# Four buffers for values, seven for gated halves, whole rows of weights, and a new order of the work, in an attention and gating kernel on one core

## The chip, the core and the metric

The kernel runs on one core of a Trainium2 chip. A core has five engines, each with its own stream of instructions: TensorE (PE in the views, its weight loads PEld), VectorE (DVE), ScalarE (ACT), GpSimd (POOL) and SyncE (SP), which here issues the DMAs. They wait for each other by semaphores alone. The metric is the device time of one execution in microseconds (us).

## The reference

Attention over B=4 batches, H=8 heads, S=768 positions and 64 elements a head, in which a query sees the first `n_global` = 8 keys and the last `n_local` = 96, with a bias that grows with distance; then a convolution of 5 taps, a sigmoid gate and two products with 512x512 weights:

```python
scores = q @ k.T / 8 - slope[h] * dist          # only kept keys
a = softmax(scores);  x = a @ v                 # heads side by side: x is [4, 768, 512]
gate = sigmoid(sum_k conv_w[k] * x[t - 4 + k])
out = (gate * (x @ w_val)) @ w_out
```

Inputs `w_val`, `w_out` and `conv_w` come as 64-bit floats, the rest and the output as 32-bit.

## The kernel before

Work is cut into 32 groups g of (batch, half of the sequence, pair of heads); a group has 3 blocks of 128 queries, in all 96 steps s. Four groups make a phase ph, a half sequence of a batch over all 512 features. For a group: `L` loads keys and queries (tile kq), `LV` loads values (va); `S` (L631) multiplies them on PE into sb; `AM` (L639) adds the bias and takes the minimum on DVE; `EX` (L650) is the exponential on ACT; `RG`, `RC` and `NM` (L657, L661, L669 or L667) divide by the sum; `PT` (L682) transposes p on PE into a PSUM bank pt or x; `EV` copies that to ab; `PV` (L709, L716) multiplies by the values, two groups at a time, into x. Then `XS` copies x to xs, `XH` and `XL` split it into a rounded and a rest part (xh, xl), `CV` (L807, L811, L809) makes the gate in five taps and `SG` (L842) its tanh. For a phase, `VM` (L849) makes val from xh, xl and the weights, three matmuls for each pair of column blocks; `GM` (L856) multiplies val by the gate; `GH` and `GL` (L863) split that into gh and gl; `OM` (L872) multiplies them with the second weights into o; `OE` (L884, L886) scales o into ob, and `ST` stores it.

The weights are taken apart from 64 to two 32-bit parts first: `WL` loads one of eight tiles of 128 rows (L534), `WA`, `WZ`, `W2` to `W4`, `WH`, `WS`, `WD` and `WP` do the arithmetic. At the end `FA`, `FB` and `FC` (L943, L947, L953 to L959) reduce the row minima to one flag: should the inputs not fit the window of this fast path, a general path runs after it. It does not run here.

Nothing is scheduled on the chip or by the framework: `SLOTS` gives each operation a number, `ENGINES` the engine for those that can run on several, and `Plan.order` writes the instructions out by that number. On an engine they run strictly in that order, SP's loads too. `plan.ring(tag, n, ...)` makes an operation that needs one of n buffers depend on the one that frees it; so `LV` of group g waits for the `PV` that used its buffer last, and `WL` of tile i for `W4` of tile i-2.

Of the kernel before, what the change touches and what calls it, by code (L numbers as in the profile page):

```python
# [17 lines left out]
RAW_B, XH_B, GATE_B, P_B, T_B, A_B, V_B, W_B, WT_B = 4, 7, 2, 7, 8, 5, 6, 2, 2  # L18
X_B, S_B, XS_B = 2, 2, 8
# [31 lines left out]
    "CWL": (14,),  # L51
    "CWA": (113,),
    "CW": (136,),
    "S0": (8,),
# [1131 lines left out]
```

## Time and profile before

| | before |
|---|---|
| median of 3 runs | 256.35 us (255.11 to 257.29) |
| profiled execution | 255.96 us, of which the span from first to last instruction is 254.2 us |
| TensorE matmuls | busy 244.3 us, 96% of the span, x3381 |
| TensorE weight loads | busy 206.1 us, x3381 |
| VectorE, ScalarE, GpSimd | busy 218.3, 197.3 and 136.2 us |
| DMA | 36.35 MB, 143 GB/s over the span |
| granted TensorE clock | 0.998 of full speed |

A busy share says how much of the time an engine had an instruction under way; matmuls overlap, so a busy PE need not be at its peak. An idle stretch of an engine is put down to what ended it ("releaser"); "issue" means that nothing the profile knows of ended it. Queue q8 in the DMA table is PE's stream of instructions, fetched from memory in packets.

### The profile page before, as it was taken

The numbers are of one execution on the slowest core, as the hardware profiler recorded it, in microseconds if no ns is written. First come the engines' busy times: TensorE is split into PE (matmuls) and PEld (weight loads), VectorE is DVE, ScalarE is ACT, GpSimd is POOL, SyncE is SP. The second block draws the span as 40 slices with busy tenths as digits, with TensorE's granted clock in tenths as the row PEclk, the third lists the DMA queues.
The fourth block names the chain that finished last, engine by engine and source line by source line (L and its number), as shares of the span: only waits on it lengthen the run. The fifth ranks groups of instructions, "written<-read, shape, count | busy, mean of one in ns | idle before, by whom it ended". The sixth has DMA issues, their size and how long they took to land.

```text
span 254.2 us, 8955 instructions
## 1 busy us (share of the span) xinstructions
PE 244.3 (96%) x3381; PEld 206.1 (81%) x3381; DVE 218.3 (86%) x768; ACT 197.3 (78%) x670; POOL 136.2 (54%) x228
## 2 busy tenths in 40 slices
PE   8898989999999999999999999999999999999992
PEld 3457757887789988899889988999899879878982
DVE  4998989999999999999999999988889777766820
ACT  4999979999998999899697989496769759333321
POOL 5797979997869554186604483055253703402110
PEclk9999999999999999999999999999999999999999
DMA  5977997736615762370826371173320003020103
GB/s 158 370 206 235 315 401 241 251 108 195 204 61 163 259 186 65 109 240 12 279 78 205 122 233 59 41 221 118 99 96 3 4 0 126 1 85 0 41 3 129
DMA packets 16302, 36.35 MB, mean 143 GB/s; under 512 B 1920, under 2 KB 4480, under 8 KB 16256
## 3 DMA queue, kind: packets, MB, share of 16 engines
q1 hardware_dynamic: 16112, 35.75, 42.3%
q8 instruction: 27, 0.44, 0.7%
q14 instruction: 19, 0.16, 0.2%
q10 hardware_dynamic: 144, 0.00, 0.0%
HBM read 29.46 MB, written 6.29 MB: 141 GB/s over the span
## 4 chain that ended last, share of the span: by engine, by line
PE 85%; ACT 5%; DVE 3%; POOL 2%; issue 1%; DMA 1%; ACTq 0%; POOLq 0%; DVEq 0%
PE val L849 27%; PE o L872 26%; PE sb L631 10%; PE x L716 9%; PE x L709 5%; PE pt L682 4%; ACT p L650 3%; PE x L682 3%; POOL p L669 1%; DMA counts_i<-in_counts 1%; ACT ab L298 1%; PE pt L544 1%; DVE t L639 1%; POOL sm L657 1%; DVE ob L886 1%
## 5 line engine op out<-in xcount | busy, mean ns | idle before, releaser
L650 ACT ACTIVATE p<-t,mins 128x168 f32<-128x168 f32 (+1 forms) x192 | 80.9, 425 | 6.3 <-PE pt L682 2.6
L807 DVE SCALAR_TENSOR_TENSOR gate<-xs,cwt,gate 128x384 f32<-128x384 f32 x128 | 82.8, 662 | 1.6 <-POOL gate L811 1.0
L639 DVE CUSTOM_DVE_ANT_0 t<-sb,bias 128x168 f32<-128x168 f32 (+1 forms) x192 | 54.5, 315 | 5.0 <-PE sb L631 4.9
L669 POOL TENSOR_SCALAR p<-p,rs 128x168 f32<-128x168 f32 (+1 forms) x86 | 49.7, 589 | 14.9 <-ACT p L650 5.7
L849 PE MATMUL val<-xh,wvh 128*128 128x384 f32 x128 | 45.2, 353 | 0.0
L849 PE MATMUL val<-xh,wvl 128*128 128x384 f32 x128 | 43.2, 337 | 0.0
L849 PE MATMUL val<-xl,wvh 128*128 128x384 f32 x128 | 43.2, 337 | 0.0
L872 PE MATMUL o<-woh,gh 128*128 128x512 f32 (+1 forms) x100 | 40.1, 401 | 0.0
L631 PEld LDWEIGHTS sb<-kq 64*64 64x64 f32 x1088 | 30.9, 134 | 10.5 <-issue 7.1
L872 PE MATMUL o<-wol,gh 128*128 128x512 f32 (+1 forms) x100 | 38.7, 387 | 0.0
L872 PE MATMUL o<-woh,gl 128*128 128x512 f32 (+1 forms) x100 | 38.5, 385 | 0.0
L631 PE MATMUL sb<-kq 64*64 64x104 f32 (+3 forms) x1088 | 36.1, 265 | 1.2 <-DMA kq<-in_kq 1.1
L650 ACT ACTIVATION_READ_ACCUMULATOR p<-t,mins 128x1 f32 x192 | 36.9, 192 | 0.0
L667 ACT ACTIVATE p<-p,rs 128x168 f32<-128x168 f32 (+1 forms) x72 | 28.8, 428 | 3.8 <-DVE rs L661 3.7
L657 POOL TENSOR_SCALAR sm<-sm 128x4 f32<-128x4 f32 (+2 forms) x30 | 9.8, 326 | 39.3 <-ACT p L650 37.0
L863 POOL TENSOR_TENSOR gl<-g,gh 128x384 fp32r<-128x384 f32 x17 | 18.5, 1091 | 16.1 <-ACT gh L298 15.7
L849 PEld LDWEIGHTS val<-xh,wvh 128*128 128x128 f32 x128 | 24.1, 188 | 2.6 <-issue 0.5
L799 POOL TENSOR_TENSOR xl<-xs,xh 128x384 fp32r<-128x384 f32 x18 | 20.2, 1120 | 9.3 <-ACT xh L298 7.8
L716 PE MATMUL x<-ab,va 104*64 104x128 f32 (+1 forms) x384 | 24.7, 277 | 0.0
L849 PEld LDWEIGHTS val<-xl,wvh 128*128 128x128 f32 x128 | 24.1, 188 | 0.4
L298 ACT COPY ab<-pt 128x384 f32<-128x384 f32 (+3 forms) x41 | 19.4, 481 | 6.1 <-PE pt L682 6.1
L849 PEld LDWEIGHTS val<-xh,wvl 128*128 128x128 f32 x128 | 24.1, 188 | 0.0
(162 smaller groups left out, 424.1 us busy)
## 6 DMA issues: line engine op xcount, KB each, us to landing
...
```

The source lines that it names most:

```text
L298: nc.scalar.copy(dst, src)
L631: nc.tensor.matmul(s[rows, u : u + w], T["rq", g][r, k * P + half * QH : k * P + (half + 1) * QH], T["rk", g][r, c : c + w], start=True, s ...
L639: nc.vector.tensor_tensor_reduce(out=t[:, :n], in0=T["s", s // HB, s % HB, j][:, :n], in1=bias[:, h, :P] if n == P else bias[:, h, P:], op ...
L650: nc.scalar.activation(T["p", s][:, j, :n], T["t", s, j][:, :n], AF.Exp, bias=mins[:, s, j : j + 1], scale=-1.0, accum_out=T["sm", batch_o ...
L667: nc.scalar.mul(pr, pr, rs)
L669: engine(e).tensor_scalar(out=pr, in0=pr, scalar1=rs, scalar2=1.0, op0=ALU.mult, op1=ALU.mult)
L716: nc.tensor.matmul(T["x", g][rows(i), c0 : c0 + P], T["near", g][:n, k, j], T["a", HB * g + k][:n, j * P : (j + 1) * P], start=False, stop ...
L799: engine(e).tensor_sub(tile_of(("xl", g), [P, HT], F32R, "xl", XH_B), xs[g % XS_B][:, HIST:], T["xh", g])
L807: nc.vector.scalar_tensor_tensor(out=gt, in0=src, scalar=w, in1=gt, op0=ALU.mult, op1=ALU.add)
L849: nc.tensor.matmul(T["val", ph, m], (wvh, wvh, wvl)[r][:, m, c * P : (c + 1) * P], (T["xh", g], T["xl", g], T["xh", g])[r], start=(c == 0 ...
L863: engine(e).tensor_sub(tile_of(("gl", ph, m), [P, HT], F32R, "gl", 5), T["g", ph, m], T["gh", ph, m])
L872: nc.tensor.matmul(T[key][:, cols], (T["gh", ph, c], T["gl", ph, c], T["gh", ph, c])[r][:, rows], (woh, woh, wol)[r][:, c, cols], start=(c ...
```

## The change

It has five parts. (1) The order `SLOTS` and the engines `ENGINES` are new numbers throughout. (2) `V_B`, the buffers for values, goes from 6 to 4, and the buffers for gh and gl from 5 to 7 (`GH_B`). (3) The first weight matrix is laid out by the host so that a tile is one whole row of 4 KB in each partition, loaded by one DMA; before, two DMAs brought four pieces of 1 KB for each partition. (4) The third instruction of `distances_all` gets a second operation (times 1.0), and the function may run on POOL as well; the table keeps it on DVE. (5) 37 of the 42 `RG`, instead of 30, run on POOL, and so on: `CV` moves 7 first taps from POOL to DVE, `EV` 11 copies, `XS` 8 and `GH` 3 from ACT to DVE, `GL` 3 from DVE to POOL, `OE` 6 from DVE to ACT, `WA` 3 from POOL to ACT; `NM` is 85 on POOL, 66 on ACT, 41 on DVE (86, 72, 34 before); `XL` is 16 on DVE (14 before).

```diff
-RAW_B, XH_B, GATE_B, P_B, T_B, A_B, V_B, W_B, WT_B = 4, 7, 2, 7, 8, 5, 6, 2, 2
-X_B, S_B, XS_B = 2, 2, 8
+RAW_B, XH_B, GATE_B, P_B, T_B, A_B, V_B, W_B, WT_B = 4, 7, 2, 7, 8, 5, 4, 2, 2
+X_B, S_B, XS_B, GH_B = 2, 2, 8, 7
...
-    "WL": (5, 9, 91, 128, 174, 255, 292, 386),
+    "WL": (5, 11, 79, 127, 167, 220, 342, 369),
...
     def distances_all(e):
-        ve = nc.vector
+        ve = engine(e)
...
-        ve.tensor_scalar(out=d1[:, G], in0=m0[:, :NG], scalar1=nlf, scalar2=None, op0=ALU.add)
+        ve.tensor_scalar(out=d1[:, G], in0=m0[:, :NG], scalar1=nlf, scalar2=1.0, op0=ALU.add, op1=ALU.mult)
...
         if i < NC:
-            t = w.rearrange("p (c n) two -> p c (n two)", c=NC)
-            src = wv.bitcast(I32).rearrange("(c p) n -> p c n", p=P)[:, :, 2 * i * P : 2 * (i + 1) * P]
-            parts = [(t[:, c], src[:, c]) for c in (slice(0, NC // 2), slice(NC // 2, NC))]
+            parts = [(w, wv[:, i].bitcast(I32).rearrange("p (n two) -> p n two", two=2))]
...
-        copy(e, tile_of(("gh", ph, m), [P, HT], F32R, "gh", 5), T["g", ph, m])
+        copy(e, tile_of(("gh", ph, m), [P, HT], F32R, "gh", GH_B), T["g", ph, m])
...
-        "wv": bits(inputs["moe_w_val"]),
+        "wv": bits(np.asarray(inputs["moe_w_val"]).reshape(NC, P, NC, P).transpose(1, 2, 0, 3)).reshape(P, NC, -1),
```

What the new numbers do at two places follows. First SP's loads near the start, from just behind the fourth weight tile on (w is a tile of weights, kq and va those of a group; the names in brackets are semaphores waited for: DMAHW of an earlier transfer, the others of an engine). Before:

```order
L393 DMA va_457<-in_va 128x640 [waits DMAHW3_49]
L379 DMA kq_481<-in_kq 128x888 [waits DMAHW4_49,PE_49]
L534 DMA w_573<-in_wo 128x512 [waits DMAHW5_49,DMAHW6_49,DVE_49,Pool_49]
L534 DMA w_573<-in_wo 128x512
L393 DMA va_607<-in_va 128x640 [waits DMAHW7_49]
L379 DMA kq_628<-in_kq 128x888 [waits DMAHW0_49,PE_49]
L379 DMA kq_635<-in_kq 128x784 [waits DMAHW1_49,PE_49]
L393 DMA va_644<-in_va 128x768 [waits DMAHW2_49]
L379 DMA kq_651<-in_kq 128x784 [waits DMAHW3_49,PE_49]
L393 DMA va_661<-in_va 128x768 [waits DMAHW4_49]
L393 DMA va_671<-in_va 128x768 [waits DMAHW5_49]
```

Of the change:

```order
L394 DMA va_440<-in_va 128x640
L380 DMA kq_474<-in_kq 128x888 [waits DMAHW0_49,PE_49]
L380 DMA kq_478<-in_kq 128x888 [waits DMAHW1_49,PE_49]
L394 DMA va_485<-in_va 128x640 [waits DMAHW2_49]
L533 DMA w_561<-in_wo 128x512 [waits DMAHW3_49,DVE_49,Pool_49]
L533 DMA w_561<-in_wo 128x512 [waits DMAHW4_49]
L380 DMA kq_576<-in_kq 128x784 [waits DMAHW5_49,PE_49]
L533 DMA w_702<-in_wo 128x1024 [waits DMAHW6_49,DVE_49,Activation_49]
L380 DMA kq_755<-in_kq 128x784 [waits DMAHW7_49,PE_49]
L380 DMA kq_762<-in_kq 128x784 [waits DMAHW0_49,PE_49]
L394 DMA va_771<-in_va 128x768 [waits DMAHW1_49]
```

Behind the fifth weight tile (the first from in_wo, in two DMAs) there are now one kq and then the sixth weight tile, w_702, which waits for DVE (`W4` of the fourth tile) and holds up what stands behind it; before, three kq and four va followed, with two more va behind the last row shown. Ahead of the fifth tile the change has one kq and one va more.

Then DVE at the end, from `GM` of the last column block (g_3) on: before, these eight are the last rows of the program there, and gl_3 is made on POOL.

```order
L856 SCALAR_TENSOR_TENSOR g_3_4567<-gate_4269,val_3_4539 128x384 [waits DVE_49,PE_49,Activation_49]
L953 TENSOR_REDUCE far<-pt_89 1x1 [waits PE_49]
L954 TENSOR_SCALAR slow<-counts 1x1
L955 SCALAR_TENSOR_TENSOR slow<-counts,slow 1x1 [waits DVE_49]
L956 SCALAR_TENSOR_TENSOR slow<-counts,slow 1x1 [waits DVE_49]
L957 SCALAR_TENSOR_TENSOR slow<-far,slow 1x1 [waits DVE_49]
L958 TENSOR_SCALAR slow<-slow 1x1 [waits DVE_49]
L959 CAST flag<-slow 1x1 [waits DVE_49]
```

Of the change, from the gl before the flag:

```order
L862 TENSOR_TENSOR gl_2_4563<-g_2_4540,gh_2_4555 128x384 [waits DVE_49,Activation_49]
L952 TENSOR_REDUCE far<-pt_89 1x1 [waits PE_49]
L953 TENSOR_SCALAR slow<-counts 1x1
L954 SCALAR_TENSOR_TENSOR slow<-counts,slow 1x1 [waits DVE_49]
L955 SCALAR_TENSOR_TENSOR slow<-counts,slow 1x1 [waits DVE_49]
L956 SCALAR_TENSOR_TENSOR slow<-far,slow 1x1 [waits DVE_49]
L957 TENSOR_SCALAR slow<-slow 1x1 [waits DVE_49]
L958 CAST flag<-slow 1x1 [waits DVE_49]
L862 TENSOR_TENSOR gl_3_4580<-g_3_4561,gh_3_4569 128x384 [waits Activation_49]
```

The seven instructions of the flag now stand ahead of the last gl on the same engine. And PE of the change at the same place, from the transposition of the minima (the matmul into pt) to the matmul that takes that gl:

```order
L946 MATMUL pt_89<-ident,row_max 1x128
L871 MATMUL o_0_4557<-woh,gh_2_4555 128x512 [waits Activation_49]
L871 MATMUL o_0_4557<-woh,gl_2_4563 128x512 [waits DVE_49]
L871 MATMUL o_0_4557<-wol,gh_2_4555 128x512
L871 MATMUL o_1_4585<-woh,gh_0_4511 128x512
L871 MATMUL o_1_4585<-woh,gl_0_4518 128x512
L871 MATMUL o_1_4585<-wol,gh_0_4511 128x512
L871 MATMUL o_0_4557<-woh,gh_3_4569 128x512 [waits Activation_49]
L871 MATMUL o_0_4557<-woh,gl_3_4580 128x512 [waits DVE_49]
```

Before, the rows are the same in kind, but the matmul that takes gl_3 comes three rows later, behind the o_1 matmuls with gh_1 and gl_1, and waits for POOL.

## Rows read from the trace of the kernel before

**Rows 1.** The page's first part: busy us (share of the span) xinstructions.

```profile
PE 244.3 (96%) x3381; PEld 206.1 (81%) x3381; DVE 218.3 (86%) x768; ACT 197.3 (78%) x670; POOL 136.2 (54%) x228
```

**Rows 2.** Stretches in us: busy time (instructions) of each engine, granted clock, DMA share, GB/s.

```profile
46.00:66.60 20.60, 20.60 (x364) 16.80 (x361) 20.60 (x82) 20.32 (x72) 18.93 (x27) 1.00 0.54 172
...
75.80:127.00 51.20, 51.17 (x820) 45.25 (x820) 50.17 (x185) 45.85 (x161) 31.13 (x49) 1.00 0.51 162
127.00:240.00 113.00, 113.00 (x1365) 99.75 (x1362) 96.25 (x292) 78.85 (x253) 40.13 (x63) 1.00 0.26 86
```

**Rows 3.** Waits of PE: line, releaser, us in total, times, longest.

```profile
PE x L709 <- ACT ab L298: 1.3, 2, 0.8
PE pt L682 <- issue: 1.3, 1, 1.3
PE x L682 <- issue: 0.3, 1, 0.3
PE x L709 <- ACT p L650: 0.2, 1, 0.2
```

**Rows 4.** PE in order of time, 33 to 36 and 42 us: start, us, operation [idle before <-releaser].

```profile
32.93 0.66 PE L682 MATMUL pt<-ident,p 64*104 64x64 f32 x11
34.85 0.21 PE L682 MATMUL pt<-ident,p 64*128 64x64 f32 x1 [1.26 <-issue]
34.99 1.22 PE L631 MATMUL sb<-kq 64*64 64x168 f32 x36
...
42.41 0.33 PE L709 MATMUL x<-ab,va 64*64 64x64 f32 x4
```

**Rows 5.** Waits of DVE, then of ACT, between 30 and 37 us.

```profile
DVE t L639 <- PE sb L631: 0.9, 1, 0.9
ACT ab L298 <- PE pt L682: 1.2, 1, 1.2
```

**Rows 6.** DMA queue q8 to 32.34 us, at 32.3 to 33.4, and to 200.68: packets, MB, share.

```profile
q8 instruction: 2, 0.03, 0.4%
...
q8 instruction: 1, 0.02, 5.4%
...
q8 instruction: 23, 0.38, 0.7%
```

**Rows 7.** Stretches from 0, columns as in rows 2.

```profile
0.00:28.50 28.50, 25.04 (x362) 15.92 (x362) 23.45 (x115) 24.22 (x94) 22.16 (x56) 1.00 0.78 244
0.00:32.35 32.35, 28.89 (x452) 19.35 (x454) 27.21 (x128) 28.07 (x107) 25.78 (x61) 1.00 0.80 260
...
0.00:200.69 200.69, 195.29 (x2988) 163.40 (x2989) 185.79 (x699) 174.49 (x613) 125.11 (x215) 1.00 0.51 169
```

**Rows 8.** DMA queue of the loads, 25.7 to 32.34 us: packets, MB, share of 16 engines.

```profile
q1 hardware_dynamic: 882, 2.20, 97.4%
```

**Rows 9.** SP in order of time, 24 to 34 us.

```profile
24.32 0.80 SPq L534 DMA_DIRECT2D w<-in_wo  x2
25.17 0.43 SPq L393 DMA_DIRECT2D va<-in_va  x1
...
27.77 5.38 SPq L393 DMA_DIRECT2D va<-in_va  x4
```

**Rows 10.** DVE's groups by form: busy us, mean ns | idle us before, releasers.

```profile
L863 DVE TENSOR_TENSOR gl<-g,gh 128x384 fp32r<-128x384 f32 x15 | 8.5, 577 | 0.0
L300 DVE COPY xs<-x 128x384 f32<-128x384 f32 x5 | 2.7, 546 | 0.0
```

**Rows 11.** PE and DVE in order of time, 242 to 245 us.

```profile
242.37 0.27 PE L947 MATMUL pt<-ident,row_max 128*1 128x128 f32 x1
...
244.12 0.39 PE L872 MATMUL o<-woh,gl 128*128 128x512 f32 x1
242.68 0.28 DVE L953 TENSOR_REDUCE far<-pt 1x1 f32<-1x128 f32 x1 [0.90 <-PE pt L947]
...
244.06 0.14 DVE L959 CAST flag<-slow 1x1 int32<-1x1 f32 x1
```

More of the change, by code (lines that the diff above doesn't have):

```diff
@@ L39 @@
-    "DIST": (10, 12),
-    "BIAS": (15, 22, 18, 25, 16, 23, 13, 36),
[10 rows of a table removed]
[L51 to L54, printed above, removed]
+    "CNT": (8,),
+    "DIST": (10, 13),
+    "BIAS": (18, 22, 15, 23, 14, 36, 16, 37),
[10 rows of a table added]
+    "CWL": (7,),
+    "CWA": (109,),
+    "CW": (135,),
+    "S0": (9,),
     "S": (
-        17, 41, 72, 107, 139, 175, 217, 259, 302, 347, 402, 439, 476, 511, 570, 630, 678, 706, 763, 810, 863, 903,
-        961, 997, 1035, 1087, 1131, 1222, 1281, 1300, 1389, 1448,
+        17, 39, 68, 98, 133, 178, 209, 245, 286, 325, 398, 438, 469, 506, 571, 595, 673, 701, 760, 806, 854, 901,
+        955, 1007, 1043, 1086, 1153, 1215, 1265, 1284, 1365, 1458,
@@ L189 @@
 ENGINES = {
-    "BIAS": "SSSVGGGG",
+    "DIST": "VV",
+    "BIAS": "SSSGGVGG",
     "BI2": "GV",
-    "WA": "GGGGGGGG",
-    "WZ": "VVGGGGGG",
-    "WH": "GSSVSSSS",
-    "WD": "VVGV",
-    "WP": "VVGVSSSS",
-    "RG": "GVGGGGGGGGGGGGVGVGVGVGGGVGGGVGGGVGGVVGVGVG",
+    "WA": "SGGSGGSG",
+    "WZ": "GGGVGGGG",
+    "WH": "GSSGSSSS",
+    "WD": "GGGV",
+    "WP": "VVVVVSSS",
+    "RG": "GGGGGGGGGGGGGGGGGVGGGGGGVGGVGGGGGGGVGGGGGV",
     "NM": (
-        "SGGVGGGGGVGSSGGGGGSGGGVGGSGSGGGSGGVGGSGVGSSGGGSSGGSGSGVGSGSGSGGSSGVGGVGVGSGGVGSGSSGGSGGVSSSGVSVS"
-        "GSSVSVSGGVVSGGSGSSSGGGGGGSSSVSSVSVSVSSVVGGSVGSSGSVGSGSSSGVSSSVSGGGVSGGGGSVVVGGGGSSGVSSGSSVVSSSSS"
-    ),
-    "EV": "SSSSSSSSSVVSSSVSSSSSVSSSSSSSSSVSSSSSSSSSSVSSSSVSSSSSSSSSVSSVSSSVVSVSVSVSSSSSVSVVSSSS",
-    "XS": "SSSSSSSSSSVSSSSVSSSVSVSSSSSSSSSV",
-    "XH": "VSSGGSGSGSSVSSGGSVGVSSVSSSVSGSGG",
-    "XL": "GVVGGGVGGGGGGGVVGGGVGVVGVVGVVGVV",
+        "VGSGGVGSSGGGGGSGGSSGVVGGGVGGVGGSGGGGGSGGSSGGGGGGGSSGGSSSVSSGGGGSSSGSGVVGVVSVSVSGSGGSGGSGVGSSVGGS"
+        "VSGSVSSSSVSGGSGGSVGVGVVSGSGGGGGSGSSGVVSSSSGGSSSSGGSSSGGSSVVGGVSGVVGVGVVSVVSGVSGSGGSGSGGSVVVVSVGV"
+    ),
+    "EV": "SVSSVSVSVVSSSSSSSSSSVSVSSSSVSSSVSSSSSSSSSSSVVSVSVSSSSSVVSVVSSVVVSSSVSSVSSVVSVSSSVSVV",
+    "XS": "SSSSSSVVSVSSVVSSSVSVVVSSSVSVVSSV",
+    "XH": "GSVVSVGGGSSSSSSGSGSSGGSSVGSVGSVS",
+    "XL": "GVVGGVGGGVVGGVGVVGGGVVVVGGGVVGVV",
     "CV": (
-        "GVVVVSVVVVSVVVVGVVVVSVVVVSVVVVGVVVVSVVVVGVVVVGVVVVSVVVVGVVVVGVVVVGVVVVVVVVVSVVVVSVVVVGVVVVGVVVVG"
-        "VVVVGVVVVSVVVVGVVVVGVVVVSVVVVGVVVVSVVVVGVVVVSVVVVGVVVVGVVVVSVVVV"
-    ),
-    "HI": "GGGGVVSVVSGGGVGG",
-    "GH": "VSSVSSSSVVSSVSVSSSSSSVSSSVSSSSSS",
-    "GL": "VGVVGVGVGGVVVGGVGGGVVGGVGVGGVVGG",
-    "OE": "VVSSVSVVSSVSVSSSVSSVSSSSS",
+        "GVVVVSVVVVSVVVVSVVVVGVVVVSVVVVGVVVVSVVVVGVVVVGVVVVSVVVVGVVVVSVVVVVVVVVVVVVVSVVVVGVVVVGVVVVSVVVVV"
+        "VVVVVVVVVSVVVVGVVVVSVVVVVVVVVSVVVVGVVVVVVVVVGVVVVSVVVVVVVVVVVVVV"
+    ),
+    "HI": "GGSGSVGGSVVVGGGS",
+    "GH": "SSSVSSSVSVSSSSVSSVVSVSSSVVSVSVSS",
+    "GL": "GGGGGVGGGGGGGVGGGVGVVVVGVGGVGVVV",
+    "OE": "SVSSSSSSSSSVSSSSSSSSSSVSS",
 }
@@ L455, in distances_all @@
     def distances_all(e):
-        ve = nc.vector
+        ve = engine(e)
         ve.tensor_scalar(out=d1, in0=rel, scalar1=nlf, scalar2=BIG, op0=ALU.is_ge, op1=ALU.mult)
         ve.tensor_add(d1, d1, rel)
-        ve.tensor_scalar(out=d1[:, G], in0=m0[:, :NG], scalar1=nlf, scalar2=None, op0=ALU.add)
+        ve.tensor_scalar(out=d1[:, G], in0=m0[:, :NG], scalar1=nlf, scalar2=1.0, op0=ALU.add, op1=ALU.mult)
     plan.add(("CNT",), (DVE,), read_counts)
     plan.add(("DIST", 0), (DVE,), distances, [("CNT",), ("IOTA",)])
-    plan.add(("DIST", 1), (DVE,), distances_all, [("DIST", 0)])
+    plan.add(("DIST", 1), (DVE, POOL), distances_all, [("DIST", 0)])
     def biases(e, h, part):
@@ L859, in g_high @@
     def g_high(e, ph, m):
-        copy(e, tile_of(("gh", ph, m), [P, HT], F32R, "gh", 5), T["g", ph, m])
+        copy(e, tile_of(("gh", ph, m), [P, HT], F32R, "gh", GH_B), T["g", ph, m])
     def g_low(e, ph, m):
-        engine(e).tensor_sub(tile_of(("gl", ph, m), [P, HT], F32R, "gl", 5), T["g", ph, m], T["gh", ph, m])
+        engine(e).tensor_sub(tile_of(("gl", ph, m), [P, HT], F32R, "gl", GH_B), T["g", ph, m], T["gh", ph, m])
     def outp(ph, k, c, half=None):
@@ L921, in attention_moe @@
             plan.add(key, (ACT, DVE), lambda e, ph=ph, m=m: g_high(e, ph, m),
-                     [("GM", ph, m)] + plan.ring("gh", 5, key, free))
+                     [("GM", ph, m)] + plan.ring("gh", GH_B, key, free))
             key = ("GL", ph, m)
             plan.add(key, (POOL, DVE), lambda e, ph=ph, m=m: g_low(e, ph, m),
-                     [("GH", ph, m)] + plan.ring("gl", 5, key, free))
+                     [("GH", ph, m)] + plan.ring("gl", GH_B, key, free))
         for k in range(HB):
```

71 lines of the change are left out of this document (35 added, 36 removed), and 132 rows, old and new, of the table SLOTS.

## The prediction

> **What bounds the kernel now.** I read the page first: PE has a matmul under way for 244.3 of 254.2 us, DVE is busy 218.3 [rows 1]. Such a share can hide stages with other limits, so I cut the span into stretches [rows 2]. From 46 to 66.6 us PE and DVE are both busy all the time and ACT nearly so: three engines in balance. From 75.8 to 127 us PE is full and DVE 50.17 of 51.2. From 127 to 240 us PE is full, DVE 96.25 of 113 and ACT 78.85 of 113: there PE alone decides. Since its matmuls are as many in the change (x3381), time can go only where PE is idle or held up, and I read its waits [rows 3]. The only long one behind no semaphore is 1.26 us, at 33.6 us, in the middle of one group of transpositions [rows 4]; a shorter one of 0.3 us is of the same kind. While PE stood, DVE waited 0.9 us for its scores and ACT 1.2 us for its transposed tile [rows 5]. PE's other waits in full work are for ACT's copies and exponentials (1.3 us in two places, 0.2 in one), where ACT itself was busy.
>
> **What that stall is.** Queue q8 brings PE's instructions. Two packets had come by 32.34 us and the third came between 32.3 and 33.4 us; 23 had come by 200.68 us and the next followed at once, on an otherwise idle queue [rows 6]. At 200.69 us PE had begun 2988 + 2989 instructions, so a packet serves 5977 / 24 = 249 of them, and the third was due at 747; PE had begun 906 when it came [rows 7]. The mark of 747 lies just behind 28.5 us (724), so the packet was some 3.5 us late, an estimate from these rows. PE stood from 33.6 us, just behind it, to 34.85. Over 25.7 to 32.34 us the queue of the loads took 97.4% of the DMA engines' time and moved 2.20 MB [rows 8], of loads that SP issued from 24.3 us on in one run: a tile of weights, kq, and values, the last four over 5.38 us [rows 9]. So I read the 1.26 us as instructions late behind data.
>
> The Trainium skill says otherwise: "Runtime: NRT & Kernel Launch", section "Instruction fetch mechanics", calls the crossing from one block of instructions to the next mostly hidden. By it the 1.26 us is something else and the change regains none of it. The trace has PE idle for 1.26 us with no semaphore outstanding, beside a fetch that came late, and the sum goes by the trace.
>
> **The change, part by part.**
>
> *Loads and buffers for values.* In the change the fifth weight tile is followed on SP by one kq and then by the sixth weight tile, which waits for DVE; in the order of before three kq and six va came there. At 2.20 MB in 6.64 us, 0.33 MB a us, the tile and one kq (0.9 MB) are through 2.7 us after 24.3, at 27 us, before the third packet is due. The stall goes. What it gives is bounded by DVE's wait (0.9) and PE's (1.26), since DVE sets the pace around it: I take 1.1. Bounds: 0, if the packet is late for another reason, and 1.26. The second packet's stall of 0.3 us [rows 3] stays in my sum: ahead of it SP now issues one kq and one va more (0.76 MB, 2.3 us at the same rate), but the weight tiles come in rows of 4 KB and not pieces of 1 KB, which the trace of before has only mixed with other loads. Bounds: -0.3, and +2.3 if the rows save nothing; I take 0, the nearest row being the stall itself.
>
> *What waits on SP behind the sixth tile.* Two kq and a va; the va serves groups 4 and 5, whose product begins at 42.41 us in the trace [rows 4], and the new numbers free the tile (`W4` of the fourth, 214) long before that product (332). Its partner va comes behind a kq that waits for the scores of group 7, over at 34.99 + 1.22 = 36.2 us [rows 4]. That leaves 6 us for a transfer, and in the change the scores of group 9 stand ahead of that product on PE. I take 0. Four SP issues fewer, the second operation in `distances_all` (once, on 8 columns) and two more buffers each for gh and gl are covered by the full engines of the first 66 us: 0.
>
> *Who does what, to 66 us.* Up to the last bias addition of group 12, DVE has 169 operations in both orders. It gains two xs copies, two large ab copies, two small ones, two rest parts of weights, one xh and one division, and loses two gl, two weight differences and some eight others. By their means (an xs copy 546 ns, a gl 577) [rows 10] the two sides differ by 0.2 us. So balance gives nothing here: +0.2, bounds 0 and +0.8 (counting from start to start in place of means). At 75.8 us PE waits 0.2 us for an exponential; the change puts that product behind other work: -0.2, bounds 0 and -0.2.
>
> *Who does what, later.* Over the whole program DVE gains 11 ab copies, 8 xs copies, 7 taps, 7 divisions, 3 gh and 2 xl and loses 6 ob, 7 guards, 3 gl and a few weight operations: +12 us by their means. From 127 to 240 us DVE idles 113 - 96.25 = 16.75 us [rows 2], so PE covers it: 0 in my sum. If that cover were gone it would be paid in part (a rival, below).
>
> *The tail.* This I can read to a tenth. Before, the flag's seven instructions run on DVE from 242.68 to 244.20 us, behind PE's transposition of 242.37, and POOL makes the last gl meanwhile. In the change that gl stands behind them on DVE. It could begin at 244.2 and needs 0.5 to 0.58 us [rows 10]: 244.7. PE wants it in the eighth matmul after the transposition, which is at 244.12 in the trace [rows 11]. PE stands 0.6 us, with seventeen or so matmuls and all of the output's end behind it, and nothing beside it: +0.6, bounds 0.5 and 0.7.
>
> *Sum.* -1.1 + 0.2 - 0.2 + 0.6 = -0.5 us. The profiled execution took 255.96 us (254.2 of span and 1.76 around it), 0.4 below the median of the runs shown: 255.5 us.
>
> **Rivals.**
>
> *More of the early waits go.* If the new order also takes away PE's 0.3 us and its waits for ACT of 1.3 us in two places, and the first stall gives its full 1.26 us, the sum is -1.26 - 0.3 - 1.3 - 0.2 + 0.6 = -2.5, or 253.5 us. For it: a wait shows that PE had nothing else in reach, and another order can give it something. Against it: DVE was full from 46 to 66.6 us, so that work done earlier on PE waits for DVE later.
>
> *The packet is late anyway.* The Trainium skill's "DMA: Bandwidth & Descriptors", section "Queues, rings and completion order", says that a DMA engine takes turns between its queues, a packet each. By that rule a fetch would not wait for a backlog of loads, and thinning them would not help. As a mechanism of this kernel: the stall of 1.26 us stays, or moves to the second packet, whose backlog grows by 0.76 MB. Then the sum is +0.2 - 0.2 + 0.6 = +0.6, or 256.6 us. Against it: a late packet in the crowded stretch, a prompt one in the empty one.
>
> *DVE becomes the bound (slower).* Place: 75.8 to 240 us. DVE has 1.0 us idle to 127 us and 16.75 behind it. If the +12 us falls in clumps, so that only half of the later idle time can take it up, 12 - 8 = 4 us come on top: 255.5 + 4 = 259.5 us. It decides once PE waits for the gate or for val's product on DVE in several phases; below 1 us added ahead of 127 us it is nothing.
>
> **How the numbers follow.** The forecast has 0.48, with a range of its own of 254.3 to 256.5 (its bounds, -1.26 to +0.8 around the terms, and the 1 us that runs of before differ by). More of the waits gone has 0.26, the late packet 0.16, DVE's bound 0.10. The range reaches from 252.7 (the second case less the scatter of 0.8) to 257.8 (the late packet with 1.2 of scatter, which is also the forecast with the second packet's bound of +2.3) and leaves the slow case out. About 1% is what a measurement here can tell from no change: 2.6 us, to 253.8 or 258.9. Faster by more: most of the second case, and a little of the first, 0.24. Slower by more: the DVE case, 0.10. Within: 0.66.
>
> **What would show it.** The first step is right if PE has no idle stretch for "issue" of over 0.5 us between 28 and 40 us and the DMA queue has a gap near 27 us; wrong, if one of about a microsecond stands there or near 25 us. The tail is right if the matmul of o with the last gl waits 0.5 to 0.7 us for DVE and DVE's flag ends just before it. The load of DVE is right if its busy time rises by about 10 us while PE stays full from 127 to 240 us. The whole is wrong if PE's waits in the first 76 us change by more than 2 us, or if it idles in the middle.

## The result, and the profile after

The change takes 257.44 us (median; 256.65 to 260.16) against 255.44 us (254.25 to 257.31) for the kernel before: a ratio of 1.0091, 95% interval 1.0071 to 1.0111. It is slower by 2.0 us, where 0.5 us less than before's profile had been forecast. The time lies in the range given and within 1% of before, but on the wrong side of no change. The profiled execution took 256.93 us with a span of 255.0.

The first part of the page, and the stretches, of the change (columns as in [rows 1, 2]):

```profile
PE 246.9 (97%) x3381; PEld 207.2 (81%) x3381; DVE 224.8 (88%) x787; ACT 191.6 (75%) x652; POOL 135.3 (53%) x227
```

```profile
46.00:66.60 20.60, 20.18 (x341) 16.41 (x341) 20.57 (x80) 19.90 (x69) 19.30 (x25) 1.00 0.55 187
...
75.80:127.00 51.20, 51.06 (x756) 44.67 (x750) 49.75 (x180) 47.12 (x163) 29.68 (x47) 1.00 0.43 136
127.00:240.00 113.00, 112.97 (x1408) 99.64 (x1400) 99.86 (x308) 72.62 (x236) 40.79 (x65) 1.00 0.30 99
```

DVE has 6.5 us more work, ACT 5.7 less. PE is still "full" from 127 to 240 us; its busy time has grown by 2.6 us with the same 3381 matmuls. A third profile of the unchanged kernel before (`before_third`, below) has 246.2 us too, so this sum says nothing of the change by itself. But a busy share can hide waits: a matmul can wait for an operand or a free PSUM tile while the one ahead is still counted as under way (rows at 185 us, near the end, show one case). PE's waits from 10 to 76 us of the change (line, releaser, us in total, times, longest), to set beside [rows 3]:

```profile
PE sb L630 <- DVE mins L638: 0.7, 1, 0.7
PE sb L630 <- DVE rs L660: 0.4, 1, 0.4
PE sb L630 <- DMA kq<-in_kq: 0.4, 1, 0.4
PE pt L681 <- POOL p L668: 0.3, 1, 0.3
...
PE x L708 <- ACT ab L299: 0.2, 1, 0.2
```

The stall of 1.26 us for instructions is gone, as forecast, and so are the waits for ACT, but for 0.2 us. Yet the time rose. To see where, I use points at which both orders have the same matmuls behind them: the product of weights and values of groups 0 and 1 (near 21 us), of groups 10 and 11 (near 76), of groups 16 and 17 (near 119), and the last matmul. The last three in `before_third` and in the change, PE in order of time:

```profile
76.20 0.69 PE L709 MATMUL x<-ab,va 64*64 64x64 f32 x32 [0.23 <-ACT p L650]
...
119.05 0.67 PE L709 MATMUL x<-ab,va 64*64 64x64 f32 x32
...
249.85 0.28 PE L872 MATMUL o<-wol,gh 128*128 128x256 f32 x1
```

```profile
75.25 0.67 PE L708 MATMUL x<-ab,va 64*64 64x64 f32 x32
...
118.75 0.67 PE L708 MATMUL x<-ab,va 64*64 64x64 f32 x32
...
250.37 0.28 PE L871 MATMUL o<-wol,gh 128*128 128x256 f32 x1
```

From 76 to 119 us before takes 119.05 - 76.20 = 42.85 us and the change 43.50; from there to the last matmul before takes 130.80 and the change 131.62. The same differences for all profiles, in us, each from such rows ("stall" is PE's idle time for "issue" between 10 and 76 us, that of the warm-up matmuls left out):

| kernel | 21 us product | to 76 | 76 to 119 | 119 to last | stall |
|---|---|---|---|---|---|
| before | 20.96 | 54.87 | 42.84 | 130.77 | 1.6 |
| before_again | 22.36 | 55.05 | 42.84 | 130.77 | 2.0 |
| before_third | 22.35 | 53.85 | 42.85 | 130.80 | 0 |
| change | 21.05 | 54.20 | 43.50 | 131.62 | 0 |
| after_again | 21.02 | 54.21 | 43.52 | 131.60 | 0 |
| tail_gl_first | 20.86 | 53.65 | 43.47 | 131.17 | 0 |
| after_waits_moved | 21.00 | 54.27 | 43.87 | 131.08 | 0 |
| after_relief | 23.25 | 53.68 | 43.84 | 130.47 | 1.1 |
| early_of_change | 23.53 | 53.52 | 43.73 | 130.74 | 0.9 |
| late_of_change | 22.49 | 53.92 | 44.26 | 131.68 | 0 |
| before_spread | 21.21 | 53.68 | 42.85 | 130.76 | 0 |
| before_rows | 21.50 | 54.60 | 42.85 | 130.77 | 1.4 |
| before_dve_4us | 21.13 | 54.44 | 42.84 | 133.20 | 1.4 |
| before_dve_4us_b | 21.14 | 55.01 | 42.84 | 132.18 | 1.9 |
| after_relief_b | 21.11 | 54.05 | 43.79 | 130.62 | 0 |
| after_engines_back | 21.98 | 53.15 | 48.99 | 135.70 | 0.8 |

Behind 76 us the three profiles of before agree within 0.05 us, and so do the two of the change, so differences of a few tenths can be read there from one profile. Ahead of 76 us executions of one kernel differ by over a microsecond, which decided this case. In `before_rows`, `after_relief`, `early_of_change` and `after_engines_back` the stall lies just ahead of the product at 21 us, not in the second column.

### The profile page after: what moved, and what is told of

The parts are those of the page before. It is cut to its first block, busy times and chain, and to the rows that moved or that the text cites. A ratio compares the mean times of both kernels' runs of the same rounds, so it can differ in the third digit from the quotient of the medians.

```text
span 255.0 us, 8953 instructions
## 1 busy us (share of the span) xinstructions
PE 246.9 (97%) x3381; PEld 207.2 (81%) x3381; DVE 224.8 (88%) x787; ACT 191.6 (75%) x652; POOL 135.3 (53%) x227
## 4 chain that ended last, share of the span: by engine, by line
PE 81%; DVE 8%; DMA 8%; issue 1%; SPq 1%; POOL 0%; ACT 0%
PE o L871 27%; PE val L848 24%; PE sb L630 11%; PE x L715 8%; DMA w<-in_wv 5%; PE pt L681 4%; PE x L708 3%; PE x L681 3%; DMA va<-in_va 2%; DVE gate L806 2%; DVE t L638 2%; PE pt L543 1%; DVE g L855 1%; SPq L387 0%; SPq L380 0%
## 5 line engine op out<-in xcount | busy, mean ns | idle before, releaser
L806 DVE SCALAR_TENSOR_TENSOR gate<-xs,cwt,gate 128x384 f32<-128x384 f32 x128 | 81.9, 655 | 0.5
L638 DVE CUSTOM_DVE_ANT_0 t<-sb,bias 128x168 f32<-128x168 f32 (+1 forms) x192 | 53.6, 316 | 4.8 <-PE sb L630 4.7
L668 POOL TENSOR_SCALAR p<-p,rs 128x168 f32<-128x168 f32 (+1 forms) x85 | 47.4, 567 | 19.6 <-DVE rs L660 13.9
L862 POOL TENSOR_TENSOR gl<-g,gh 128x384 fp32r<-128x384 f32 x20 | 22.8, 1141 | 39.5 <-ACT gh L299 23.3
L630 PEld LDWEIGHTS sb<-kq 64*64 64x64 f32 x1088 | 32.7, 135 | 10.5 <-issue 5.9
L630 PE MATMUL sb<-kq 64*64 64x104 f32 (+3 forms) x1088 | 39.0, 268 | 1.9 <-DVE mins L638 0.7
L656 POOL TENSOR_SCALAR sm<-sm 128x4 f32<-128x4 f32 (+2 forms) x37 | 13.1, 354 | 33.8 <-ACT p L649 27.7
L666 ACT ACTIVATE p<-p,rs 128x168 f32<-128x168 f32 (+1 forms) x66 | 26.8, 424 | 1.7 <-DVE rs L660 1.6
L883 ACT ACTIVATE ob<-o 128x512 f32<-128x512 f32 (+1 forms) x22 | 12.4, 573 | 14.1 <-PE o L871 14.0
L841 ACT ACTIVATE gate<-gate 128x384 f32<-128x384 f32 x32 | 16.5, 522 | 8.5 <-DVE gate L806 8.4
```

What stands on the lines that cost most here:

```text
L630: nc.tensor.matmul(s[rows, u : u + w], T["rq", g][r, k * P + half * QH : k * P + (half + 1) * QH], T["rk", g][r, c : c + w], start=True, s ...
L638: nc.vector.tensor_tensor_reduce(out=t[:, :n], in0=T["s", s // HB, s % HB, j][:, :n], in1=bias[:, h, :P] if n == P else bias[:, h, P:], op ...
L666: nc.scalar.mul(pr, pr, rs)
L668: engine(e).tensor_scalar(out=pr, in0=pr, scalar1=rs, scalar2=1.0, op0=ALU.mult, op1=ALU.mult)
L806: nc.vector.scalar_tensor_tensor(out=gt, in0=src, scalar=w, in1=gt, op0=ALU.mult, op1=ALU.add)
L841: nc.scalar.activation(gt, gt, AF.Tanh, scale=0.5)
```

## Experiments

**The tail, the two halves of the order, and the run of loads.** `tail_gl_first`, on the change:

```diff
-        1440, 1443, 1470, 1474, 1560, 1564, 1573, 1583, 1629, 1643, 1649, 1654,
+        1440, 1443, 1470, 1474, 1560, 1564, 1573, 1583, 1629, 1643, 1649, 1653,
...
-    "FC": (1653,),
+    "FC": (1654,),
```

> The changed kernel with one swap in the order: the last gl (phase 7, third value tile) goes to DVE ahead of the flag's seven instructions, not behind them. If the tail's term is right, the wait of 0.33 us (0.56 from start to start) of PE for that gl goes and nothing else moves: 0.3 to 0.5 us less than the change, about 257.0 us, still slower than before by about 1.5. If the flag is on the path that sets the end, the time rises by up to 0.5 us instead. This run is also a second profile of everything else in the change: if the 2.0 us between the medians come from loads that vary from run to run, its waits in the first 50 us will differ from those of the first profile by over 0.5 us.

Measured: 257.47 us, ratio 1.0087 (1.0056 to 1.0118). In the trace the term is there: 119 us to the last matmul takes 131.17 us in place of 131.62 and 131.60, 0.44 less. The interval of the ratio is too wide to show it in the times. In the change, DVE and PE at the tail:

```profile
242.86 0.27 PE L946 MATMUL pt<-ident,row_max 128*1 128x128 f32 x1
...
244.26 0.14 DVE L958 CAST flag<-slow 1x1 int32<-1x1 f32 x1
244.33 0.54 DVE L862 TENSOR_TENSOR gl<-g,gh 128x384 fp32r<-128x384 f32 x1
...
244.92 0.19 PEld L871 LDWEIGHTS o<-woh,gl 128*128 128x128 f32 x1 [0.60 <-DVE gl L862]
```

The gl starts as the flag ends and PE waits for it: what [rows 11] had led me to expect. PE lost 0.44 us, not 0.60: the weight load waited for 0.60 us, but ran beside an earlier matmul.

`early_of_change` and `late_of_change` take their tables from one kernel up to the work that PE does at 76 us and from the other behind it. One row of each, the engines of the xs copies (first against the change, then against before):

```diff
-    "XS": "SSSSSSVVSVSSVVSSSVSVVVSSSVSVVSSV",
+    "XS": "SSSSSSVVSVVSSSSVSSSVSVSSSSSSSSSV",
...
-    "XS": "SSSSSSSSSSVSSSSVSSSVSVSSSSSSSSSV",
+    "XS": "SSSSSSSSSSSSVVSSSVSVVVSSSVSVVSSV",
```

> The changed kernel up to the work that PE does at 76 us (order, engines, whole-row weights, four value buffers), and behind that the order and engines of before (the later loads of values moved back as far as four buffers require). Theory A, the loss is behind 76 us, where DVE has more work and PE waits for its scores: op by op the first 76 us of the change gain 0.3 to 0.8 us, so 254.6 to 255.1 us. Theory B, the loss is in the early loads and copies: 257 us or more.

> The kernel before up to the work that PE does at 76 us, with its six value buffers, five gated halves and weights in pieces, and behind that the order and engines of the change. Theory A: the waits of the change behind 76 us (0.6 us near 98, 0.8 near 185, 0.4 in the tail, and some tenths) come here too, 256.8 to 257.3 us, and PE waits near 185 us for DVE. Theory B: 255.4 to 255.9 us, the tail's wait alone.

Measured: 256.46 us, ratio 1.0053 (1.0029 to 1.0077), and 257.97 us, 1.0089 (1.0055 to 1.0124). The first lies between the ranges of the two theories, the second above that of theory A, and neither number is pure: at the seam, at 84 and 80 us, the hybrids wait for scores that neither parent waits for (0.47 us for DVE's minima in the one, 0.70 in the other), which is in their 76 to 119 us (43.73 and 44.26). Behind 119 us the table is clean: the last part of the change costs 131.68 us also behind the head of before, and the last part of before 130.74 also behind the head of the change. So the loss behind 119 us belongs to the order and engines there, as theory A says. It does not belong to the numbers of buffers: `early_of_change` has the change's four for values and seven for gh and gl, `late_of_change` has before's six and five. Theory A's other half failed: the head of the change brought no gain.

`before_spread`, SP's order before and now:

```diff
-L393 DMA va_644<-in_va 128x768
-L379 DMA kq_651<-in_kq 128x784
-L393 DMA va_661<-in_va 128x768
-L393 DMA va_671<-in_va 128x768
-L393 DMA va_681<-in_va 128x768
-L393 DMA va_785<-in_va 128x640
-L534 DMA w_803<-in_wo 128x1024
+L534 DMA w_791<-in_wo 128x1024
+L393 DMA va_793<-in_va 128x768
+L379 DMA kq_795<-in_kq 128x784
...
```

> The kernel before with six loads moved in SP's order alone: five loads of values and one kq go from ahead of the sixth weight tile to behind it, so that the run of loads from 24.3 us is cut from 2.2+ MB to about 1.7 MB and ends earlier. If the third instruction packet is late behind the loads, it comes by 31 us, PE's 1.26 us of idle time at 33.6 us goes, and the time falls by 0.9 to 1.2 us to 254.3. If a packet is late whatever the loads do, the 1.26 us stays: 255.4. If the loads moved back become late themselves, PE waits for values near 42 us: 255.4 to 257.

Measured: 256.23 us, ratio 1.0016 (0.9990 to 1.0043). In its profile the third packet came by 28.5 us, PE had no stall, and the execution took 254.86 us. By that profile alone the term of 1.1 us was right; by the times it was worth nothing. The two can both hold if the stall comes and goes between executions of the same program, which is what the next runs asked.

**Is the stall in every execution?** `before_again`, `before_third` and `after_again` are the two kernels unchanged. `before_rows`, on before:

```diff
-            t = w.rearrange("p (c n) two -> p c (n two)", c=NC)
-            src = wv.bitcast(I32).rearrange("(c p) n -> p c n", p=P)[:, :, 2 * i * P : 2 * (i + 1) * P]
-            parts = [(t[:, c], src[:, c]) for c in (slice(0, NC // 2), slice(NC // 2, NC))]
+            parts = [(w, wv[:, i].bitcast(I32).rearrange("p (n two) -> p n two", two=2))]
```

> The kernel before, unchanged, for a second profile. My main term rested on one profile, in which the third instruction packet came 7.4 us behind its trigger and PE stood for 1.26 us. If that belongs to the order of the loads, the stall is there again within 0.3 us. If it belongs to that execution alone (the kernel that keeps this head and changes only what comes behind 76 us had the packet in time), PE has no idle stretch of over 0.5 us for issue between 28 and 40 us, and the term was worth nothing for a typical run. Time: 255.4 us, ratio 1.000.

> The kernel before unchanged, a third profile. Both earlier ones are from executions above the median (255.96 and 257.43 against 255.4) and both have PE's 1.3 us of idle time behind the third instruction packet. If the stall belongs to the order of the loads, it is here again, whatever the time. If it belongs to the slower executions, a run of 255.2 us or less has none.

> The change unchanged, a second profile. Between the first profiles of the two kernels the difference is 1.0 us, between their medians 2.0. Either the first profile of the change was of a quick execution: then this one takes 257.4 us or more, and the added time stands ahead of 76 us (loads that land late, or PE's instruction packets), since what follows 76 us was alike within 0.3 us in all profiles of the change. Or both profiles are typical, 256.9, and the difference to the medians is the kernel before having been slow in its profile.

> The kernel before with one part of the change: the first four weight tiles are stored so that each is one transfer of whole 4 KB rows in place of two of 1 KB pieces; the order stays. My term for it was nothing: 255.2 to 255.7 us. If the pieces cost transfer time, the tiles land sooner, the copies that wait for them start sooner, and the instruction packets with them: down to 254.5. If one transfer of 4 KB rows lands later than two halves (the first half can be used by nobody before the second, but queues are shared with kq), 256 us or more.

Measured: `before_again` 256.63 us, ratio 1.0023 (0.9994 to 1.0052); `before_third` 256.19 us, 0.9988 (0.9955 to 1.0022); `after_again` 257.40 us, 1.0085 (1.0048 to 1.0122), its profiled execution 256.94; `before_rows` 256.64 us, 1.0034 (1.0008 to 1.0060). A kernel against itself came out at 1.0023 here, so 1.0034 for the whole rows is not told apart from nothing.

PE's waits from 10 to 76 us in `before_again`, then in `before_third`, the same program (of the second a warm-up row is left out):

```profile
PE x L709 <- ACT ab L298: 1.6, 2, 1.1
PE pt L682 <- issue: 1.3, 1, 1.3
PE x L682 <- issue: 0.7, 1, 0.7
PE sb L631 <- DVE mins L639: 0.2, 1, 0.2
```

```profile
PE x L709 <- ACT ab L298: 1.3, 2, 1.1
PE sb L631 <- PE pt L682: 0.3, 1, 0.3
PE sb L631 <- DVE mins L639: 0.2, 1, 0.2
...
```

And PE's instruction queue: in `before_again` to 33.8 and to 34.9 us, in `before_third` to 27.5 and to 29.5 us (packets, MB, share):

```profile
q8 instruction: 2, 0.03, 0.4%
...
q8 instruction: 3, 0.05, 0.5%
```

```profile
q8 instruction: 2, 0.03, 0.5%
...
q8 instruction: 3, 0.05, 0.7%
```

The order of the loads is the same, yet the third packet came between 33.8 and 34.9 us in one execution and between 27.5 and 29.5 in the other, and the stall of 1.3 us with it or not. Already the first packet tells which it will be: it had come by 15 us in `before_third`, `before_spread` and `late_of_change`, and in all three PE has no stall; it had not come by 16 us in the two other profiles of before, in `before_dve_4us` and in `before_dve_4us_b`, and in all four PE stalled between 33 and 37 us, for 1.26, 1.3, 0.93 and 1.5 us. To 15 us in `before_third` (in before this queue has no row up to 16.9 us):

```profile
q8 instruction: 1, 0.02, 0.4%
```

The change has both kinds too: the first packet by 15 us and no stall in its two profiles, but not by 18.9 us in `after_relief`, where PE waits at 20 us:

```profile
PE sb L630 <- issue: 1.1, 1, 1.1
```

`early_of_change` has 0.9 us at the same place, `before_rows` 1.4 and `after_engines_back` 0.8. In all sixteen profiles the two go together: the first packet by 15 us and no stall in eight, not by 16 us and a stall in eight. So the stall comes and goes between executions, in both kernels. In before it is worth 1.0 to 1.2 us of the 21 to 76 us of before (54.87 and 55.05 against 53.85). What decides how early the first packet comes is not shown here. (A packet of q14, another queue of instructions, comes at 13.1 to 15.4 us in every profile; PE's first is ahead of it in the eight without a stall and behind it in the others.)

The prediction's reading of the loads is borne out in one point. Where the first packet is late, the third comes between 32.3 and 33.9 us with before's loads, but at 30.2 and 30.8 us in `after_relief` and `early_of_change`, with the change's, and PE does not stand behind it there. But in these two PE has already stood 1.1 and 0.9 us at 21 us, beside a first packet that came at 19.0 and 19.5 us. There the stall did not go; it moved ahead and became shorter.

The keys of group 1 vary in the same way: PE's first scores of that group start at 7.84 us in before, at 9.38 in `before_third`, at 7.79 and 7.67 in the two profiles of the change. An execution of before with early keys and early packets would take 256.49 - 1.5 = 255.0 us (256.49 is the profiled execution of `before_third`; an estimate, from these rows), near its median; `before_spread`, with keys at 7.93 us and no stall, took 254.86. The change with both early took 256.93 and 256.94. Like with like the change costs some 1.9 us, and the medians say 2.0. My first two profiles had set an execution of before with late packets beside one of the change without.

**Is it the places, or DVE's work?** `after_waits_moved` mends four places. The tail is as in `tail_gl_first`; on DVE the minimum of step 89 goes up 14 places; one `NM` of step 85 goes from POOL to ACT; two `NM` of step 46 go up one place, one on DVE and one on POOL. The last of these, POOL's order:

```diff
 L668 TENSOR_SCALAR p_1994<-p_1994,rs_2035 128x168
+L668 TENSOR_SCALAR p_1907<-p_1907,rs_2035 128x168
 L810 TENSOR_SCALAR gate_1820<-xs_84,cwt 128x384
-L668 TENSOR_SCALAR p_1907<-p_1907,rs_2035 128x168
```

> The change with four places mended, those where PE waits behind 76 us in both of its profiles: the tail's gl ahead of the flag; the minimum of step 89 on DVE moved up 14 places, so that PE's scores of group 30 do not wait for it near 185 us; one normalised tile of step 85 from POOL to ACT; two of step 46 one place earlier on DVE and POOL. Theory A1 (the loss is in these few places, which the order puts late on DVE and POOL): PE's waits of 0.5 near 98, 0.7 near 185 and 0.3 in the tail go, 1.3 to 1.6 us less, 255.9 to 256.2. Theory A2 (DVE's added work is the cause, and a wait removed comes back at the next product): at most 0.5 us less, 257.0 to 257.4.

`after_engines_back`, on the change, here three of its rows of engines:

```diff
-    "XS": "SSSSSSVVSVSSVVSSSVSVVVSSSVSVVSSV",
+    "XS": "SSSSSSVVSVVSSSSVSSSVSVSSSSSSSSSV",
...
-    "GH": "SSSVSSSVSVSSSSVSSVVSVSSSVVSVSVSS",
+    "GH": "SSSVSSSSVVSSVSVSSSSSSVSSSVSSSSSS",
...
-    "OE": "SVSSSSSSSSSVSSSSSSSSSSVSS",
+    "OE": "SVSSVSVVSSVSVSSSVSSVSSSSS",
```

> The change with its order kept, and behind the work of 76 us every operation on the engine that it had before (205 operations move; DVE's busy time falls by about 4 us behind 76 us). Theory A2: the waits of PE behind 76 us go although the order is the new one, 255.9 to 256.5. Theory A1: the order was made for other engines, new waits appear in other places, 257.5 to 260.

Measured: `after_waits_moved` 258.06 us, 1.0103 (1.0066 to 1.0140), the time of neither theory. The waits went where they were mended; behind 119 us 0.5 us was gained (131.08), nearly all of it the tail's, and from 76 to 119 us 0.37 was lost (43.87). A new wait, at 109 us, as one row of PE's waits says:

```profile
PE val L848 <- ACT ob L883: 0.3, 1, 0.3
```

`after_engines_back`: 266.41 us, 1.0398 (1.0356 to 1.0441). PE's longest waits in it:

```profile
PE pt L681 <- DVE p L668: 1.6, 2, 1.3
PE pt L681 <- ACT p L666: 1.6, 1, 1.6
PE pt L681 <- POOL p L668: 1.5, 2, 1.1
```

An order and its engines belong together: with the old engines the new order has a normalised tile late on every one of three engines. That run says nothing on DVE's amount of work, so two others changed that and kept the order. `after_relief` is `after_waits_moved` with 16 more operations from DVE to ACT (here two of five rows):

```diff
-    "XS": "SSSSSSVVSVSSVVSSSVSVVVSSSVSVVSSV",
+    "XS": "SSSSSSVVSVSSVVSSSVSSSVSSSSSVVSSS",
...
-    "GH": "SSSVSSSVSVSSSSVSSVVSVSSSVVSVSVSS",
+    "GH": "SSSVSSSVSVSSSSVSSVSSVSSSSSSSSSSS",
```

> The change with the four places mended as before, and 16 further operations behind 100 us (copies, high halves, normalisations; about 6.5 us of work) taken from DVE to ACT, each at a point where ACT stood idle in the trace of the change. Mending the four places alone took PE's waits there away, 0.9 us, and 0.8 came back near 106, 108 and 193 us. Theory A2 (DVE's added work is what PE waits for behind 76 us, wherever it shows): with DVE lighter the waits of PE behind 100 us fall and stay away, 0.5 to 1.0 us from the work of 76 us to the end less than the change, 256.4 to 257.0; what is left is near 92 to 108 us, where ACT has no room. Rival (the order of the change costs it, whoever does the work): the same sum of waits, 257.4 or more.

`before_dve_4us`, on before, both rows that differ:

```diff
-    "EV": "SSSSSSSSSVVSSSVSSSSSVSSSSSSSSSVSSSSSSSSSSVSSSSVSSSSSSSSSVSSVSSSVVSVSVSVSSSSSVSVVSSSS",
+    "EV": "SSSSSSSSSVVSSSVSSSSSVSSSSSSSSSVSSSSSSSSSSVSSSSVSSSSSSSVSVVVVSSVVVSVVVSVSSVSSVSVVSSSS",
...
-    "GH": "VSSVSSSSVVSSVSVSSSSSSVSSSVSSSSSS",
+    "GH": "VSSVSSSSVVSSVSVSSVSSVVSSVVSSSSSS",
```

> The kernel before with its order kept and nine operations behind 128 us moved from ACT to DVE: six copies of ab and three high halves of gated values, all of which the change also gives to DVE. That adds 6 x 0.55 + 3 x 0.35 = 4.4 us to DVE's 95.2 of 112 us between 128 and 240 us, as much as the change adds there. Theory A2 in its simple form (the amount of DVE's work decides, though it fits into its idle time): 0.5 to 1.0 us more from PE's product at 76 us to the end, with waits of PE for DVE behind 128 us; 256.0 to 256.5. Rival (the amount alone is covered by the 16.8 us that DVE idles; what costs is where the new order puts it): the stretch from 76 us to the end stays at 173.4 to 173.5 us, and the time at that of before within 0.3 us.

Measured: `after_relief` 257.20 us (255.01 to 259.56), 1.0027 (0.9991 to 1.0062), its profile one with a late first packet. Behind 119 us it takes 130.47 us, 1.1 less than the change and 0.3 less than before. Against `after_waits_moved`, which has the same order, it is 0.61 less, so that much belongs to the 16 operations, as theory A2 has it. DVE's row there is back to what it was (128 to 240 us; in the change 99.65, in before 95.25):

```profile
128.00:240.00 112.00, 112.00 (x1409) 98.80 (x1408) 95.01 (x295) 80.00 (x255) 40.26 (x65) 1.00 0.31 100
```

`before_dve_4us`: 258.23 us, 1.0088 (1.0059 to 1.0117). Nine operations moved, 4.4 us of work, cost 133.20 - 130.78 = 2.4 us behind 119 us, more than twice what theory A2 had said. So the amount is not covered, and something else is in it. PE fell 1.4 us behind between 172 and 178 us: two sets of scores that start at 172.62 and 175.66 us in before start at 172.87 and 177.34 here. PE's order of time there, and a little earlier DVE's and POOL's:

```profile
174.67 0.33 PE L709 MATMUL x<-ab,va 64*64 64x64 f32 x4 [0.34 <-DVE ab L300]
175.26 0.68 PE L709 MATMUL x<-ab,va 64*64 64x64 f32 x28 [0.27 <-DVE ab L300]
...
169.94 1.08 POOL L863 TENSOR_TENSOR gl<-g,gh 128x384 fp32r<-128x384 f32 x1
170.07 1.17 DVE L300 CAST gh<-g 128x384 fp32r<-128x384 f32 x1
...
171.61 1.00 POOL L863 TENSOR_TENSOR gl<-g,gh 128x384 fp32r<-128x384 f32 x1
171.67 1.16 DVE L300 CAST xh<-xs 128x384 fp32r<-128x384 f32 x1
```

The moved gh, 0.35 us where nothing of POOL's runs beside it, took 1.17 us, to just behind POOL's gl; and since it had pushed the next split xh under the next gl, that took 1.16 us, which in before took 0.67. DVE stood while POOL worked. The minima of DVE, which read scores from PSUM, keep their 0.32 us beside POOL's work; it is operations on tiles in SBUF that stand. Both kernels have such places. In the change, at 91.5 us:

```profile
91.55 1.42 DVE L806 SCALAR_TENSOR_TENSOR gate<-xs,cwt,gate 128x384 f32<-128x384 f32 x1
91.55 1.00 POOL L862 TENSOR_TENSOR gl<-g,gh 128x384 fp32r<-128x384 f32 x1
```

The Trainium skill has this rule ("SBUF — State Buffer", section "SBUF: two separate sides"): VectorE and GpSimd share a pair of ports; when a VectorE operation runs in a two-port mode, or has two inputs from SBUF while GpSimd's operation reads SBUF, the one that starts first holds the pair to its end and the other blocks. These rows agree: the tap has two inputs from SBUF, and the three long operations of DVE end 0.2 to 0.4 us behind POOL's. In which mode the casts ran no row shows.

Two last runs ask how much of the cost is the amount and how much such places. `before_dve_4us_b`, against `before_dve_4us`, and `after_relief_b`, of which one row of engines against `after_relief` (its other edit takes the two moves of step 46 back):

```diff
-    "EV": "SSSSSSSSSVVSSSVSSSSSVSSSSSSSSSVSSSSSSSSSSVSSSSVSSSSSSSVSVVVVSSVVVSVVVSVSSVSSVSVVSSSS",
+    "EV": "SSSSSSSSSVVSSSVSSSSSVSSSSSSSSSVSSSSSSSSSSVSSSSVSSSSSSSVSVVVVSVVVVSVVVSVSSVSSVSVVSSSS",
...
-    "GH": "VSSVSSSSVVSSVSVSSVSSVVSSVVSSSSSS",
+    "GH": "VSSVSSSSVVSSVSVSSSSSVVSSVVSSSSSS",
```

```diff
-    "GL": "GGGGGVGGGGGGGVGGGVGVVVVGVGGVGVVV",
+    "GL": "GGGGGVVGGGGGGVGGGVGVVVVGVGGVGVVV",
```

> As the run that moved nine operations from ACT to DVE, but one of them is another: the high half of phase 4's second value tile stays on ACT, and a copy of ab (step 68) goes to DVE in its place, so that DVE has 4.6 us more and not 4.4. In that run this high half took 1.17 us on DVE and not 0.35, beside POOL's gl (169.94 to 171.03), and the next split of x 1.16 us beside the next gl; PE fell 1.7 us behind between 168 and 178 us. Theory L (DVE stands while POOL runs a two-operand operation, if its own operation reads from SBUF; an operation moved into such a place costs up to 0.8 us more than its length): 119 us to the last matmul falls from 133.2 to 131.3 to 131.8. Theory A2 (the amount of DVE's work): 133.0 or more, since the amount has grown.

> As the run that took 16 operations off DVE, with two differences: the two tiles of step 46 stay where the change has them (moving them had put a tap of the gate beside POOL's rest part of x at 105 us, where it took 1.25 us and not 0.61), and one gl of phase 1 goes from POOL to DVE (beside it, a tap at 91.5 us took 1.42 us). Theory L: 76 to 119 us falls from 43.84 to 42.9 to 43.3, and 119 us to the last matmul stays at 130.5, so that behind 76 us the kernel is level with before (173.65) or 0.2 us better. Theory A2: DVE has more work there, so 43.5 or more. The time: 255.4 to 256.3 us, by the first packets of the execution.

Measured: `before_dve_4us_b` 257.36 us, 1.0066 (1.0032 to 1.0099); `after_relief_b` 256.79 us, 1.0044 (1.0018 to 1.0071). With slightly more work on DVE but without those two places, 119 us to the last matmul takes 132.18 us: 1.0 of the 2.4 us went with these places, at which DVE had stood 1.3 us beside POOL (0.82 and 0.49), and 1.4 is left. That lies between the theories, nearer L. The 1.4 us were not taken apart: amount and place are both in them.

`after_relief_b` refutes my reading of 76 to 119 us. The tap at 91.5 us shrank as expected, to 0.59 us without the gl beside it:

```profile
91.43 0.59 DVE L806 SCALAR_TENSOR_TENSOR gate<-xs,cwt,gate 128x384 f32<-128x384 f32 x1
```

and yet the stretch takes 43.79 us and not 43.3 or less. Undoing the moves of step 46 did not take the other tap, at 105 us, from beside POOL's xl: it took 1.25 us again. Behind 119 us it takes 130.62, a little less than before. No version here is shown to be faster than the kernel before.

## Why the prediction was wrong, step by step

*The stall and its cause.* That the third packet was late and PE stood for it is right for the execution that was profiled. The failed step is "The stall goes. What it gives ... I take 1.1", in a sum compared with other executions: the stall is in two of three profiles of before, and absent in the third and in `late_of_change`, which keeps before's loads ahead of 76 us. The change shows the same two kinds of execution. Between like executions the term was near nothing. From group 1's first scores to the product at 76 us, executions without a stall take 66.8 to 67.0 us with before's loads (`before_spread` among them) and 67.1 to 67.8 with the change's; those with a stall take 67.7 to 68.3 and 67.5 to 68.0. So, with all that differs ahead of 76 us, the change gains some 0.2 us where the first packet is late, not 1.1, and loses 0.1 to 1.0 where it is in time. My only lower bound of 0 was "if the packet is late for another reason"; that it might be late in one execution and in time in the next I had not considered. The Trainium skill's sentence ("Runtime: NRT & Kernel Launch", "Instruction fetch mechanics"), that the crossing is mostly hidden, agrees with the executions whose first packet comes by 15 us; in the others one or two crossings were not hidden and cost 0.8 to 2.0 us. The rival that the packet is late anyway was nearer: in executions with a late first packet the stall moved to an earlier packet. Its reason was not tested.

*DVE's later work.* "+12 us ... PE covers it: 0 in my sum" is the other failed step. Of the 12 us by means 6.5 show in DVE's busy time. From 127 to 240 us it rose by 3.6 us, well below the 16.75 us that it idled, and still the stretch from 119 us on lost 0.38 us besides the tail. The work comes in bursts, and the operation that PE wants can be at a burst's end. At 185 us in the change, PE and then DVE:

```profile
185.11 0.75 PE L681 MATMUL pt<-ident,p 64*104 64x64 f32 x12
185.78 1.54 PE L630 MATMUL sb<-kq 64*64 64x168 f32 x34
...
185.21 0.67 DVE L806 SCALAR_TENSOR_TENSOR gate<-xs,cwt,gate 128x384 f32<-128x384 f32 x1
185.80 0.32 DVE L638 CUSTOM_DVE_ANT_0 t<-sb,bias 128x168 f32<-128x168 f32 x1
```

The scores of group 30 need the sb tile that this last minimum frees; from their first matmul to the next operation's takes 1.3 us, against 0.9 in before (189.43 to 190.33). The rival of DVE as a bound had named the mechanism, but asked for PE's waits of 4 us and said that it "decides once PE waits for the gate or for val's product". It waited for minima and normalised tiles, tenths of a microsecond at a time. Mending single places did little: with those of steps 85 and 89 mended, `after_waits_moved` gained 0.09 of the 0.38 us. Taking 16 operations off DVE besides gained 0.61.

*From 76 to 119 us.* I had "below 1 us added ahead of 127 us it is nothing". DVE's busy time did not rise there (50.17 to 49.75 us), yet 0.65 us was lost, part of it near 98 us, where PE waits for two tiles of step 46. Mending that place on DVE and POOL (43.87), or taking the gl from beside a tap (43.79), did not help, so the cause of these 0.65 us stays open.

*The tail.* +0.6 was forecast with bounds of 0.5 and 0.7, and 0.44 measured, since part of the wait ran beside an earlier matmul; the mechanism holds. Behind the waiting matmul stood 34 more, not seventeen or so, which changes nothing in the term.

*The first 66 us.* DVE's balance was put at +0.2, bounds 0 and +0.8. From 21 to 76 us, between executions without stall, the change takes 54.20 against 53.85, +0.35 (one profile, `tail_gl_first`, has 53.65). Ahead of that, from group 1's first scores to the product at 21 us, it takes 13.26 and 13.35 against 12.97, though other profiles with before's loads have up to 13.29. The 0.2 us for an exponential at 75.8 us went, as forecast. The other waits for ACT that the change removes came back as waits for DVE and POOL.

*The sum as measured.* 0.3 + 0.35 + 0.65 + 0.44 + 0.38 = 2.1 us between like executions, against 2.0 between the medians. The first two terms come from few executions that differ by several tenths, so their size is an estimate; the last three repeat within 0.05 us. The whole rows show no effect that these runs can tell from nothing, and the numbers of buffers none behind 119 us; ahead of that no run changed the buffers alone.
